# Four edits to the order of the work in a gated mix of dilated attention and a squared-ReLU MLP

## The chip, the cores and the metric

The kernel runs on one core of one Trainium2 chip. A core has a matrix engine (TensorE, PE in the profile, whose weight loads are shown apart as PEld), a vector engine (VectorE, DVE), a scalar engine (ScalarE, ACT), GpSimd (POOL), and SyncE (SP), which here does nothing but issue the transfers (DMAs) between the memories. The metric is the time of one launch on the device in microseconds (us), the median of several runs.

## What is computed

The input x has 2,048 rows (tokens) of 448 numbers. One branch is attention with 16 heads of 28 numbers, in which a token sees itself and seven earlier ones at every second place; the other is an MLP with 1,792 hidden columns and a squared ReLU. A gate per token mixes them:

```python
qkv = (x @ wqkv).reshape(B, S, 3, H, Dh)               # H = 16, Dh = 28
off = jnp.arange(8) * 2                                # a window of 8, dilation 2
logits = einsum("bhsd,bhswd->bhsw", q, k[s - off]) * Dh ** -0.5
a = einsum("bhsw,bhswd->bhsd", softmax(logits), v[s - off]) @ wo
h = x @ w1 + b1
b = relu(h) ** 2 @ w2 + b2
g = sigmoid((x * gate_w).sum(-1))
out = g * a + (1 - g) * b
```

All of it is float32, and so are the operands on TensorE. Each operand is split into a high part that is rounded (ScalarE writes it) and a low part, the difference (VectorE subtracts). A product is then three: high by high, high by low, low by high.

## The kernel before

**Tiling and stages.** The tokens are taken in four chunks of 512. First comes the product with wqkv, chunk by chunk, which also makes the sum under the gate as one more column of v. Chunk 0 is `qkv_first`. Chunk 1 is two calls of `qkv_two`, one for each two tiles of 128 tokens. Chunk 2 is `qkv_seven`, which makes q and k by seven products where eight are usual; it needs sums and differences of the chunk's tokens, which `token_sums(2)` makes on VectorE and then splits into parts. Chunk 3 is again two calls of `qkv_two`, and into the second of them the first products of the MLP (h) are put. Then the MLP runs over the chunks in the order 3, 0, 1, 2 (products called h and b), and the product with wo closes the attention.

**Row halves.** The inner dimension is cut into halves of 64 rows. Two products, one of the lower and one of the upper 64 rows, run side by side on TensorE, each into its own accumulator (a bank of PSUM); 63 such pairs make one call of `qkv_two`. When both accumulators of two such products are through with their first half, they change places: what ran in the lower rows now runs in the upper. Before that, `turn` makes VectorE write one element into each of the two banks (L212), in a column that holds no result. The write waits for the products so far and the next products wait for the write, so it sets the halves' order. In `qkv_two` the list of steps says after how many pairs each turn stands. In chunk 2 the function `turned` (L360) writes in the same way.

**What sets the order.** No scheduler chooses; the program is written under `tc.manual_schedule()`, and instructions go to each engine's queue in the order in which Python issues them. That order follows a planned clock. `advance(dt)` adds the planned time of some products to `clock["pe"]` and then issues whatever is due: `when(t, fn)` puts work at a planned time of the whole run, `at(dt, fn)` at a time from now, and `soon` is 1,500 ns from now (`LO_DELAY`), used for low parts, which so go to VectorE some time behind ScalarE's high part. Planned times (in ns) are not measured ones: each engine takes its queue in order and waits for what it needs.

**Attention** is a generator with its own planned clock, which `advance` keeps beside that of the products. It has eight units: two halves of the tokens (par) by four groups of four heads (g). For a unit, GpSimd makes eight products of q and k (`qk_piece`, L561), and VectorE sums each over a head's 28 numbers (L562); after the softmax GpSimd makes eight products with v (L568), and VectorE sums them (L576). GpSimd's products go through four buffers in turn (`PP_BUFS`). The unit's q, k and v are loaded from memory (`att_load_qk`, L532 and L533, and `att_load_v`, L538), to which `stage_store` (L235) has written them after ScalarE's copies of the accumulators into the staging tiles st (L243). After unit 0's loads, the generator lets `ATT_DELAY` ns of planned time pass.

**MLP weights.** W1 comes in four pieces. `w1_piece(i, dt, gap)` has SyncE load a piece into one of the two buffers `w1raw` (L754), and places the splits of its four parts at the planned times dt, dt + gap and so on. Pieces 0 and 1 are split straight (L130 on ScalarE, L131 on VectorE) into w1ah and w1al, and the last, short part into w17h and w17l. Pieces 2 and 3 (w1bh, w1bl) and the first rows of W2 (`w2_piece`, w2ah, w2al) go another way: ScalarE writes the high part (L740) and a copy of the raw rows into a PSUM bank (L741), and VectorE subtracts from that copy (L746). There is one copy tile, so ScalarE's next copy waits for VectorE's subtraction.

**SyncE** issues all transfers in one queue. An issue that waits (a store for its st tile, a load for the store before it) holds back all that stand behind it.

Of the kernel before, what the change touches and what calls it, by code (L numbers as in the profile page):

```python
# [33 lines left out]
QK_FIRST = 2130.0  # L34
AV_COST = 2000.0
SM_COST = 600.0
ATT_DELAY = 17000.0
LO_DELAY = 1500.0
HL_DELAY = 1800.0
COPY_DELAY = 1300.0  # L40
# [17 lines left out]
def gated_mix_kernel(ctx: ExitStack, tc: tile.TileContext, xT, wqkv, w1, w2, wo, b1, b2, out):  # L58
# [70 lines left out]
    def split_full(raw, hi, lo, soon=now):  # L129
        nc.scalar.activation(hi, raw, AF.Copy)  # L130
        soon(lambda: nc.vector.tensor_sub(lo, raw, f32(hi)))  # L131
# [117 lines left out]
    def full(x, acc, tl, b, ks=range(3)):  # L249
        sl, n = slice(tl * P, tl * P + P), block(b)  # L250
        r = []
        for k in ks:
            r += [(acc, x.h[k][:, sl], wqh[:, k, n]), (acc, x.h[k][:, sl], wql[:, k, n]),
                  (acc, x.l[k][:, sl], wqh[:, k, n])]
        return r

    def last(x, acc, tl, b):

        sl = slice(tl * P, tl * P + P)
        n = slice(D, D + NV) if b == 2 else slice(0, D)  # L260
        h, l = w7h[:, n], w7l[:, n]
        return [(acc, x.x7[:, sl], h), (acc, x.x7[:, sl], l), (acc, x.x8[:, sl], h)]

    def accs(c, b, tls, tags):
        return [Acc(t, f"qkv{c}_{tl}_{b}", NV if b == 2 else D) for t, tl in zip(tags, tls)]
# [43 lines left out]
    def qkv_two(x, c, t0, beside=(), copies=False):  # L309

        t1 = t0 + 1
        kinds = ("mm", "bm", "bb") if beside else ("mm", "mb", "bb")
        (q0, q1), (k0, k1), (v0, v1) = (accs(c, b, (t0, t1), tags) for b, tags in enumerate(kinds))
        if copies:
            copy_tile()

        parts = []
        for ends in (True, False):
            for one, two in (((q0, t0, 0), (k1, t1, 1)), ((q1, t1, 0), (k0, t0, 1)), ((v0, t0, 2), (v1, t1, 2))):
                r = [full(x, *o) + (last(x, *o) if ends else []) for o in (one, two)]  # L320
                parts.append(r if ends else r[::-1])
        run(c, [sum((p[r] for p in parts), []) for r in range(2)],
            [(24, [], (q0, k1)), (36, [], (q1, k0)), (42, [], (v0, v1)), (45, [(0, t0, q0), (1, t1, k1)]),
             (51, [], *beside[:1]), (54, [(0, t1, q1), (1, t0, k0)]), (57, [], *beside[1:]),
             (63, [(2, t0, v0), (2, t1, v1)])])

# [46 lines left out]
    class Group:  # L373
# [12 lines left out]
        def token_sums(self, n, j):  # L386
            a, b = sums[self.c, (None, 1, 0, 0, 1)[n]], (None, 1, 0, 1, 0)[n]
            o = (2 * self.u + b) * P if j < 2 else CH + b * P
            return tuple(t[:, o:o + P] for t in a)
# [146 lines left out]
    def att_load_v(par, g, tag="v"):  # L536
        v = kv_tile(tag, f"v{par}{g}")
        nc.sync.dma_start(v, halo_ap(v_d, par, g))  # L538
        return v
# [87 lines left out]
    def attention():  # L627
# [18 lines left out]
        for i in range(n + 1):  # L646
            if i < n:
# [5 lines left out]
                if i == 0:  # L653
                    vs[0] = att_load_v(par, g)
                    yield ATT_DELAY
                lgs[i] = smp.tile([P, NS, W, HG], F32, tag="lg", name=f"lg{i}")
# [71 lines left out]
    def copy_tile():  # L728


        assert not copy[1]
        copy[0] = ps("b", f"copy{len(later)}")
# [188 lines left out]
    def when(t, fn, *args):  # L921
        later.append((t, lambda: fn(*args)))
# [39 lines left out]
    def token_sums(c):  # L962
        raw = xraw[c]
        add, sub = nc.vector.tensor_add, nc.vector.tensor_sub

        def r(j, i):
            return raw[j].rearrange("p (u t n) -> p u t n", u=2, t=2)[:, :, i]

        def made(a):
            one, two = a, a + 1  # L970
            return [lambda: (add(r(two, 1), r(two, 1), r(one, 1)), sub(r(one, 1), r(one, 0), r(one, 1))),
                    lambda: (sub(r(one, 0), r(two, 1), r(one, 0)), sub(r(two, 0), r(two, 0), r(one, 0)))]

        def begin():
            for j in range(2):
                sums[c, j] = [halfp.tile([P, FA], F32R, tag=f"e{2 * j + n}", name=f"s{c}_{j}{'hl'[n]}")[:, 48:48 + CH + 2 * P]
                              for n in range(2)]

        def cut(j):
            split_full(raw[j], *(t[:, :CH] for t in sums[c, j]), soon)  # L980
            for u, rows in enumerate((LOW, HIGH)):
                split_full(raw[2 + j][rows, u * 2 * P:(u + 1) * 2 * P], *(t[rows, CH:] for t in sums[c, j]), soon)
        return made(0) + made(2) + [lambda: (begin(), cut(1)), lambda: cut(0)]

    def steps(t, gap, fns):
        for i, fn in enumerate(fns):
            when(t + i * gap, fn)
# [43 lines left out]
            when(t + 5000.0, lambda c: x_spill(c, xs[c]), c)  # L1031
    when(23500.0, x_more, 2)
    when(39500.0, x_more, 3)
    when(42500.0, lambda: steps(42600.0, 850.0, token_sums(2)))
    when(10500.0, x_spill, 0, x)
    when(25000.0, w1_piece, 0, 38000.0, 2000.0)
    when(44500.0, halos)
    when(46500.0, w1_piece, 1, 58500.0, 1500.0)
    when(66800.0, w1_piece, 2, 76300.0, 1400.0)
    when(67800.0, w1_piece, 3, 82000.0, 1400.0)  # L1040
    for j in range(2):
# [20 lines left out]
    qkv_first(xs[0])  # L1062
    qkv_two(xs[1], 1, 0)
    qkv_two(xs[1], 1, 2)
    st_["spilled"] = 0
    clock["on"] = True
    clock["att"] = clock["pe"] - 1.0
# [422 lines left out]
```

## Time and profile before

| | us |
|---|---|
| median of 3 runs | 414.14 (414.07 to 414.32) |
| the profiled execution | 414.31 |
| its span, from the first instruction to the last | 412.5 |
| TensorE busy | 407.3 (99%) |
| TensorE's weight loads busy | 391.0 (95%) |
| VectorE busy | 278.9 (68%) |
| GpSimd busy | 267.8 (65%) |
| ScalarE busy | 220.5 (53%) |

All times inside the span are counted from its start. Chunk 1's first half runs from 30.6 us, its second from 43.4, chunk 2 from 56.4, chunk 3's first half from 80.1; the MLP's first products (h) come in from 104.0. In a row of the timeline stand the start, the length in us, the engine, the line, the operation, the tiles (what is written, then what is read) with their shapes and types, the count of instructions that the row holds, and in brackets a wait with what ended it.

### The profile page before, as it was taken

The numbers are of one execution on the slowest core, as the hardware profiler recorded it, in microseconds if no ns is written. First come the engines' busy times: TensorE is split into PE (matmuls) and PEld (weight loads), VectorE is DVE, ScalarE is ACT, GpSimd is POOL, SyncE is SP. The second block draws the span as 40 slices with busy tenths as digits, with TensorE's granted clock in tenths as the row PEclk, the third lists the DMA queues.
The fourth block names the chain that finished last, engine by engine and source line by source line (L and its number), as shares of the span: only waits on it lengthen the run. The fifth ranks groups of instructions, "written<-read, shape, count | busy, mean of one in ns | idle before, by whom it ended". The sixth has DMA issues, their size and how long they took to land.

```text
span 412.5 us, 9366 instructions
## 1 busy us (share of the span) xinstructions
PE 407.3 (99%) x3817; PEld 391.0 (95%) x3817; DVE 278.9 (68%) x454; ACT 220.5 (53%) x498; POOL 267.8 (65%) x167
## 2 busy tenths in 40 slices
PE   8999999999999999999999999999999999999997
PEld 7999999989899998999999999999999999998996
DVE  4674865575857767686765897878676677792344
ACT  4674877476875555445565435354553254346640
POOL 0000000967699999979998898999989978950000
PEclk9999999999999999999999999999999999999999
DMA  7999899979272504654020679865136430158304
GB/s 216 359 370 330 254 373 277 371 229 328 97 252 84 207 11 171 209 184 153 2 85 0 206 235 265 242 153 153 43 136 224 193 129 0 39 154 151 108 2 180
DMA packets 67020, 74.00 MB, mean 179 GB/s; under 512 B 33504, under 2 KB 59296, under 8 KB 66848
## 3 DMA queue, kind: packets, MB, share of 16 engines
q1 hardware_dynamic: 66976, 73.39, 55.7%
q8 instruction: 30, 0.49, 0.5%
q14 instruction: 14, 0.11, 0.1%
HBM read 45.94 MB, written 28.25 MB: 180 GB/s over the span
## 4 chain that ended last, share of the span: by engine, by line
PE 93%; DVE 3%; DMA 1%; ACT 1%; issue 1%; SPq 0%; DVEq 0%; ACTq 0%
PE h L202 32%; PE b L202 31%; PE qkv L202 15%; PE a L202 7%; PE v L344 2%; PE qkv L291 2%; PE x L344 1%; DVE lg L562 1%; DMA xraw<-xT 1%; PE a L1262 1%; PE z L344 1%; DVE st L437 1%; PE y L344 1%; PE w L344 1%; DVE o L576 0%
## 5 line engine op out<-in xcount | busy, mean ns | idle before, releaser
L561 POOL TENSOR_TENSOR qk<-q,k 128x896 f32<-128x896 f32 x64 | 134.7, 2139 | 86.5 <-DMA k<-k_d 76.9
L568 POOL TENSOR_TENSOR av<-lg,v 128x896 f32<-128x896 f32 x64 | 118.9, 1963 | 3.2 <-DVE lg L562 2.8
L860 DVE TENSOR_TENSOR h<-h,h 128x512 fp32r<-128x512 f32 x56 | 38.6, 689 | 61.3 <-ACT h L863 60.8
L202 PE MATMUL b<-w2ah,h 64*128 64x448 f32 x448 | 74.6, 359 | 0.0
L202 PE MATMUL b<-w2bh,h 64*128 64x448 f32 x448 | 73.2, 360 | 0.4 <-DVE h L860 0.4
L576 DVE TENSOR_REDUCE o<-av 128x112 f32<-128x896 f32 x64 | 66.7, 1069 | 0.9 <-POOL av L568 0.9
L562 DVE TENSOR_REDUCE lg<-qk 128x32 f32<-128x896 f32 x64 | 67.0, 1074 | 0.0
L202 PE MATMUL qkv<-wqh,x 64*128 64x448 f32 (+1 forms) x384 | 61.6, 362 | 0.6 <-DVE qkv L212 0.6
L861 ACT ACTIVATE h<-h,b1z 128x512 f32<-128x512 f32 x56 | 36.7, 655 | 42.9 <-PE h L202 42.9
L202 PEld LDWEIGHTS b<-w2ah,h 64*128 64x128 f32 x448 | 58.9, 184 | 0.3
L202 PEld LDWEIGHTS b<-w2bh,h 64*128 64x128 f32 x448 | 55.1, 184 | 1.6 <-DVE h L860 0.7
L202 PE MATMUL b<-w2al,h 64*128 64x448 f32 x224 | 54.7, 358 | 0.0
L202 PE MATMUL b<-w2bl,h 64*128 64x448 f32 x224 | 51.8, 359 | 0.0
L202 PEld LDWEIGHTS qkv<-wqh,x 64*128 64x128 f32 x384 | 45.4, 185 | 2.7 <-DVE qkv L212 1.1
L202 PE MATMUL qkv<-wql,x 64*128 64x448 f32 (+1 forms) x192 | 44.7, 361 | 0.0
L862 ACT ACTIVATE h<-h 128x512 fp32r<-128x512 f32 x56 | 33.5, 598 | 1.7
L202 PEld LDWEIGHTS b<-w2al,h 64*128 64x128 f32 x224 | 34.2, 184 | 0.1
L863 ACT ACTIVATE h<-h 128x512 f32<-128x512 f32 x56 | 33.3, 594 | 0.0
L202 PEld LDWEIGHTS b<-w2bl,h 64*128 64x128 f32 x224 | 31.6, 184 | 0.4
L808 ACT ACTIVATE h<-h 128x4 fp32r<-128x4 f32 (+1 forms) x35 | 7.2, 207 | 45.0 <-PE b L202 44.9
L202 PEld LDWEIGHTS qkv<-wql,x 64*128 64x128 f32 x192 | 25.5, 185 | 0.7
L243 ACT ACTIVATE st<-qkv 128x448 f32<-128x448 f32 x36 | 18.0, 542 | 11.1 <-PE qkv L202 8.0
(261 smaller groups left out, 940.1 us busy)
## 6 DMA issues: line engine op xcount, KB each, us to landing
k<-k_d SPq DMA_DIRECT2D x8, 840.0 KB, 6.1
v<-v_d SPq DMA_DIRECT2D x8, 840.0 KB, 4.9
x_d<-x SPq DMA_DIRECT2D x12, 512.0 KB, 7.6
q_d<-st SPq DMA_DIRECT2D x8, 448.0 KB, 6.5
k_d<-st SPq DMA_DIRECT2D x8, 448.0 KB, 6.2
w1raw<-w SPq DMA_DIRECT2D x4, 896.0 KB, 9.7
q<-q_d SPq DMA_DIRECT2D x8, 448.0 KB, 3.6
o_d<-o SPq DMA_DIRECT2D x16, 224.0 KB, 2.7
```

The source lines that it names most:

```text
L202: nc.tensor.matmul(acc.pt[:, :acc.n], a[rows], w[rows], start=acc.todo == acc.all, stop=acc.todo == 1)
L243: nc.scalar.activation(st[:, :, t % 2], heads(pt), AF.Copy)
L291: nc.tensor.matmul(acc.pt[:, :D], a, w, start=k == j == 0, stop=False)
L344: nc.tensor.matmul(self.pt[:, :self.n], a, w, start=new, stop=True, skip_group_check=True)
L561: nc.gpsimd.tensor_mul(pr, q[:, s:s + 1].to_broadcast([P, W, C]), k[:, s:s + W])
L562: pending.append(lambda: nc.vector.tensor_reduce(lg[:, s], pr.rearrange("p w (h d) -> p w h d", h=HG), axis=AX.X, op=ALU.add))
L568: nc.gpsimd.tensor_mul(pr.rearrange("p (h d) w -> p w h d", h=HG), lg[:, s][:, :, :, None].to_broadcast([P, W, HG, DH]), v[:, s:s + W].rea ...
L576: nc.vector.tensor_reduce(o[:, g * C:(g + 1) * C], pr, axis=AX.X, op=ALU.add)
L860: nc.vector.tensor_sub(hl, pt, f32(hh))
L861: ops += [lambda pt=pt, r=r: nc.scalar.activation(pt, pt, AF.Relu, bias=b1t[:, f + r:f + r + 1]), lambda pt=pt, hh=hh: nc.scalar.activatio ...
L862: lambda pt=pt, hh=hh: nc.scalar.activation(hh, pt, AF.Square),
L863: lambda pt=pt, r=r, low=low: (nc.scalar.activation(pt, pt, AF.Square), at(delays[r], low))]
```

## The change

Four edits, none of which adds or removes an instruction:

1. `ATT_DELAY` falls from 17,000 to 16,000 ns: attention's plan runs 1 us ahead of where it was, against the products.
2. In `qkv_two` the turn of q1 and k0 stands after 30 pairs, not 36. The products themselves keep their places.
3. `token_sums` now returns two lists: the sums, which stay at 42,600 ns and every 850 from there, and the splits (`cut`), which were the last two steps of that row (46,000 and 46,850) and now stand at 50,300 and 51,700.
4. The second piece of W1 is no longer put at 46,500 ns. It is called after the second `qkv_two` of chunk 1, so that its transfer stands behind that half's stores of q, k and v. Its splits keep their planned times (58,500 and every 1,500).

```diff
--- before.py
+++ after.py
@@ -34,7 +34,7 @@
 QK_FIRST = 2130.0
 AV_COST = 2000.0
 SM_COST = 600.0
-ATT_DELAY = 17000.0
+ATT_DELAY = 16000.0
 LO_DELAY = 1500.0
 HL_DELAY = 1800.0
 COPY_DELAY = 1300.0
@@ -320,7 +320,7 @@
                 r = [full(x, *o) + (last(x, *o) if ends else []) for o in (one, two)]
                 parts.append(r if ends else r[::-1])
         run(c, [sum((p[r] for p in parts), []) for r in range(2)],
-            [(24, [], (q0, k1)), (36, [], (q1, k0)), (42, [], (v0, v1)), (45, [(0, t0, q0), (1, t1, k1)]),
+            [(24, [], (q0, k1)), (30, [], (q1, k0)), (42, [], (v0, v1)), (45, [(0, t0, q0), (1, t1, k1)]),
              (51, [], *beside[:1]), (54, [(0, t1, q1), (1, t0, k0)]), (57, [], *beside[1:]),
              (63, [(2, t0, v0), (2, t1, v1)])])
 
@@ -980,7 +980,7 @@
             split_full(raw[j], *(t[:, :CH] for t in sums[c, j]), soon)
             for u, rows in enumerate((LOW, HIGH)):
                 split_full(raw[2 + j][rows, u * 2 * P:(u + 1) * 2 * P], *(t[rows, CH:] for t in sums[c, j]), soon)
-        return made(0) + made(2) + [lambda: (begin(), cut(1)), lambda: cut(0)]
+        return made(0) + made(2), (lambda: (begin(), cut(1)), lambda: cut(0))
 
     def steps(t, gap, fns):
         for i, fn in enumerate(fns):
@@ -1031,11 +1031,15 @@
             when(t + 5000.0, lambda c: x_spill(c, xs[c]), c)
     when(23500.0, x_more, 2)
     when(39500.0, x_more, 3)
-    when(42500.0, lambda: steps(42600.0, 850.0, token_sums(2)))
+
+    def sums_begin():
+        made, cuts = token_sums(2)
+        steps(42600.0, 850.0, made)
+        steps(50300.0, 1400.0, cuts)
+    when(42500.0, sums_begin)
     when(10500.0, x_spill, 0, x)
     when(25000.0, w1_piece, 0, 38000.0, 2000.0)
     when(44500.0, halos)
-    when(46500.0, w1_piece, 1, 58500.0, 1500.0)
     when(66800.0, w1_piece, 2, 76300.0, 1400.0)
     when(67800.0, w1_piece, 3, 82000.0, 1400.0)
     for j in range(2):
@@ -1062,6 +1066,7 @@
     qkv_first(xs[0])
     qkv_two(xs[1], 1, 0)
     qkv_two(xs[1], 1, 2)
+    w1_piece(1, 58500.0, 1500.0)
     st_["spilled"] = 0
     clock["on"] = True
     clock["att"] = clock["pe"] - 1.0
```

TensorE's queue is the same as before. On GpSimd one low part of W2 stands behind the third of attention's products with v instead of ahead of it. VectorE's, ScalarE's and SyncE's queues differ at many places; the three below are those of the following text.

**SyncE, end of chunk 1.** The rows L1015 are stores of zeros ahead of the tokens, L754 is the second piece of W1, L235 are the stores of the second half of chunk 1 (each holds two token tiles), L532 and L533 the loads of q and k for attention's unit 0. Before:

```order
L1015 DMA v_d<-halo_128 8x7x112
L754 DMA w1raw_844<-w 128x4x448
L235 DMA q_d<-st_2_0_861 128x4x224
L235 DMA k_d<-st_3_1_863 128x4x224
L235 DMA v_d<-st_2_2_911 128x4x224
L532 DMA q_917<-q_d 128x896
L533 DMA k_918<-k_d 128x1680
```

Now:

```order
L1015 DMA v_d<-halo_128 8x7x112
L235 DMA q_d<-st_2_0_849 128x4x224
L235 DMA k_d<-st_3_1_851 128x4x224
L235 DMA v_d<-st_2_2_900 128x4x224
L754 DMA w1raw_906<-w 128x4x448
L532 DMA q_908<-q_d 128x896
L533 DMA k_909<-k_d 128x1680
```

The piece has moved past three stores; the loads of attention's unit 0 stand behind all four in both. On ScalarE, in the same stretch, the splits of the sums (s_1h, s_0h, three rows each) stood ahead of the first copy of q; now s_1h stands behind the four copies of q and k, and s_0h behind the two of v.

**VectorE, chunk 3, first half.** The MEMSET rows in twos are turns; the names qkv_1_0, qkv_0_1 and so on give the token tile and then 0, 1 or 2 for q, k or v. L746 is a low part made from the copy tile, L562 a sum of attention. Before:

```order
L746 TENSOR_TENSOR w17l<-copy_1275,w17h 64x64
L746 TENSOR_TENSOR w1bl_1329<-copy_1275,w1bh_1326 128x448
L562 TENSOR_REDUCE lg_1169<-qk_4_1333 128x32
L212 MEMSET qkv_1_0_1270 1x1
L212 MEMSET qkv_0_1_1271 1x1
L746 TENSOR_TENSOR w1bl_1327<-copy_1275,w1bh_1324 128x448
L562 TENSOR_REDUCE lg_1169<-qk_5_1347 128x32
L212 MEMSET qkv_0_2_1273 1x1
L212 MEMSET qkv_1_2_1274 1x1
```

Now:

```order
L746 TENSOR_TENSOR w17l<-copy_1275,w17h 64x64
L562 TENSOR_REDUCE lg_1159<-qk_4_1333 128x32
L212 MEMSET qkv_1_0_1270 1x1
L212 MEMSET qkv_0_1_1271 1x1
L746 TENSOR_TENSOR w1bl_1329<-copy_1275,w1bh_1326 128x448
L746 TENSOR_TENSOR w1bl_1327<-copy_1275,w1bh_1324 128x448
L562 TENSOR_REDUCE lg_1159<-qk_5_1347 128x32
L212 MEMSET qkv_0_2_1273 1x1
L212 MEMSET qkv_1_2_1274 1x1
```

The turn of q1 and k0 has moved past one low part. Ahead of v's turn stand the same rows as before.

**VectorE, chunk 3, second half.** Here the low parts are those of W2's first rows (w2al), and the sum of qk_0 is the first of attention's unit 1. Before:

```order
L212 MEMSET qkv_2_0_1488 1x1
L212 MEMSET qkv_3_1_1491 1x1
L746 TENSOR_TENSOR w2al<-copy_1494,w2ah 128x448
L562 TENSOR_REDUCE lg_1169<-qk_7_1405 128x32
L212 MEMSET qkv_3_0_1489 1x1
L212 MEMSET qkv_2_1_1490 1x1
L746 TENSOR_TENSOR w2al<-copy_1494,w2ah 128x448
L212 MEMSET qkv_2_2_1492 1x1
L212 MEMSET qkv_3_2_1493 1x1
L746 TENSOR_TENSOR w2al<-copy_1494,w2ah 128x448 x2
L562 TENSOR_REDUCE lg_1441<-qk_0_1547 128x32
```

Now:

```order
L212 MEMSET qkv_2_0_1488 1x1
L212 MEMSET qkv_3_1_1491 1x1
L212 MEMSET qkv_3_0_1489 1x1
L212 MEMSET qkv_2_1_1490 1x1
L746 TENSOR_TENSOR w2al<-copy_1494,w2ah 128x448 x2
L562 TENSOR_REDUCE lg_1159<-qk_7_1405 128x32
L562 TENSOR_REDUCE lg_1441<-qk_0_1547 128x32
L212 MEMSET qkv_2_2_1492 1x1
L212 MEMSET qkv_3_2_1493 1x1
L746 TENSOR_TENSOR w2al<-copy_1494,w2ah 128x448 x2
```

The turn of q1 and k0 now stands ahead of the first low part. The two sums stand together between the second low part and v's turn, where there was one between the first and the second low part and one behind the fourth.

## The prediction

> **What bounds the kernel now.** I read the page first, then the waits of the weight loads on TensorE, then single stretches of the timeline where those waits lie.
>
> ```profile
> span 412.5 us, 9366 instructions
> PE 407.3 (99%) x3817; PEld 391.0 (95%) x3817; DVE 278.9 (68%) x454; ACT 220.5 (53%) x498; POOL 267.8 (65%) x167
> ```
>
> TensorE (PE) is busy 407.3 of 412.5 us. The change leaves its 3,817 products alone, word for word in the same order, so it can move the time only through the holes between them. The profiled execution took 414.31 us, 1.8 us more than its span and 0.17 us above the median of 414.14; I add shifts of the span to the median. What TensorE's weight loads waited for, from the whole span:
>
> ```profile
> PEld qkv L202 <- DVE qkv L212: 1.1, 2, 0.9
> PEld b L202 <- DVE h L860: 0.7, 1, 0.7
> PEld h L202 <- ACT st L243: 0.2, 1, 0.2
> ```
>
> Inside the span there are four small holes: two behind VectorE's one-element writes (L212, the "turns" that the change moves), one behind a low part of the MLP at 371 us, one behind a copy at 104 us. That is the ground on which the change can gain. For the two turns:
>
> ```profile
> 30.63 0.42 PE L202 MATMUL qkv<-wqh,x 64*128 64x448 f32 x2
> ...
> 43.36 0.42 PE L202 MATMUL qkv<-wqh,x 64*128 64x448 f32 x2
> ...
> 56.41 0.37 PE L344 MATMUL v<-wqh,x 64*128 64x450 f32 x2
> ...
> 88.99 0.37 PE L202 MATMUL qkv<-wqh,x 64*128 64x448 f32 x2
> 89.92 0.47 PE L202 MATMUL qkv<-wqh,x 64*128 64x448 f32 x2 [0.56 <-DVE qkv L212]
> 90.22 0.37 PE L202 MATMUL qkv<-wql,x 64*128 64x448 f32 x2
> ```
>
> The first half of chunk 1 takes 43.36 - 30.63 = 12.73 us, the second, with the same products, 56.41 - 43.36 = 13.05: its hole costs 0.3. At 89 us a pair follows each 0.20 us; the pair due at 89.19 runs as from 90.02 (its successor is at 90.22): 0.83 lost. So 1.1 us hang on the two late turns.
>
> **The change, part by part.**
>
> *The turn of q1 and k0, six pairs sooner.* In chunk 1 it now stands before a 0.62 us low part and two sums, and nothing waits: 0.3 us gained there. In chunk 3's first half this is VectorE's row of work, with the product that follows:
>
> ```profile
> 86.36 1.13 DVE L746 TENSOR_TENSOR w17l<-copy,w17h 64x128 fp32r<-64x128 f32 x4
> 88.17 0.62 DVE L746 TENSOR_TENSOR w1bl<-copy,w1bh 128x448 fp32r<-128x448 f32 x1 [0.68 <-ACT copy L741]
> 88.71 1.08 DVE L562 TENSOR_REDUCE lg<-qk 128x32 f32<-128x896 f32 x1
> 89.72 0.64 DVE L746 TENSOR_TENSOR w1bl<-copy,w1bh 128x448 fp32r<-128x448 f32 x1
> 89.78 0.06 DVE L212 MEMSET qkv<- 1x1 f32 x2
> 90.29 1.07 DVE L562 TENSOR_REDUCE lg<-qk 128x32 f32<-128x896 f32 x1
> 91.31 0.64 DVE L746 TENSOR_TENSOR w1bl<-copy,w1bh 128x448 fp32r<-128x448 f32 x1
> 91.37 0.06 DVE L212 MEMSET qkv<- 1x1 f32 x2
> ...
> 91.83 0.36 PE L202 MATMUL qkv<-wqh,x 64*128 64x450 f32 x2
> ```
>
> The turn ended at 89.84 and TensorE went on as from 90.02, so 0.18 us pass from one to the other. Now the low part (w1bl) goes behind the turn: the reduction runs from 87.50, the turn at 88.6, due by 89.19 - 0.18 = 89.01. That hole closes, 0.83. But v's turn, the second pair of writes at 91.37, still stands behind the same instructions: the reduction (to 88.55), the turn, w1bl (to 89.2), ScalarE's refill of the one copy tile (0.6, to 89.8), w1bl (to 90.4), a reduction (1.0), so it ends at 91.50, against 91.43 now. v's products, then due 0.83 sooner, start at 91.50 + 0.18 = 91.68 instead of 91.83. The gain here is 0.15, not 0.83; VectorE's queue hands it back 1.8 us later.
>
> *Token sums' splits behind the copies.* ScalarE now copies q and k first, which lets their stores go about 1 us sooner:
>
> ```profile
> 53.42 1.38 ACT L130 ACTIVATE s_0h<-xraw 128x512 fp32r<-128x512 f32 x3
> 54.82 2.39 ACT L243 ACTIVATE st<-qkv 128x448 f32<-128x448 f32 x5
> ...
> 55.21 1.47 DVE L131 TENSOR_TENSOR s_0l<-xraw,s_0h 128x512 fp32r<-128x512 f32 x3
> ...
> 60.11 0.36 PE L344 MATMUL v<-wqh,x 64*128 64x450 f32 x2
> ```
>
> The last four of the moved rows end up behind v's copies, so near 59.3 rather than 54.8, and VectorE's low parts (1.47 us) near 59.9. Queued behind them is the turn of chunk 2's first v, due at 60.11 - 0.3 - 0.18 = 59.6. I price that at 0.3 us, between nothing (if ScalarE is 0.3 sooner) and 0.5; it eats the gain of chunk 1's turn. It does not enter the sum, because the next part fixes TensorE's place anew.
>
> *The second piece of W1 behind the stores.* The costly part. SyncE's issues, and the time to landing of the piece issued at 53.70:
>
> ```profile
> 53.70 0.60 SPq L754 DMA_DIRECT2D w1raw<-w  x1
> ...
> 57.75 1.61 SPq L235 DMA_DIRECT2D v_d<-st  x1
> 64.29 0.33 SPq L532 DMA_DIRECT2D q<-q_d  x1
> 65.65 0.33 SPq L533 DMA_DIRECT2D k<-k_d  x1
> 66.98 0.32 SPq L538 DMA_DIRECT2D v<-v_d  x1
> ...
> DMA to landing us min/median/max: 9.2/9.2/9.2
> ```
>
> The three loads at 64.29, 65.65 and 66.98 each waited for one store to land. So the transfers land one after the other in the order of issue: the piece at 62.9, then q, k and v about 1.35 us apart. With the piece last, the three stores come before it and it lands near 62.9 + 3 x 1.35 = 66.9, at the most where v landed, 66.98; if v's store is smaller or overlaps, not below 66.3. I take 66.6. [...] Who waits for the piece:
>
> ```profile
> 65.19 1.51 ACT L130 ACTIVATE w1ah<-w1raw 128x448 fp32r<-128x448 f32 x3
> ...
> 65.81 0.63 DVE L131 TENSOR_TENSOR w1al<-w1raw,w1ah 128x448 fp32r<-128x448 f32 x1 [0.52 <-ACT w1ah L130]
> 66.38 1.16 DVE L437 TENSOR_TENSOR st<-y,st 128x448 f32<-128x448 f32 x2
> 67.45 0.62 DVE L131 TENSOR_TENSOR w1al<-w1raw,w1ah 128x448 fp32r<-128x448 f32 x1
> 68.20 0.06 DVE L360 MEMSET x<- 1x1 f32 x1
> ...
> 69.17 0.36 PE L344 MATMUL x<-w2ah,s_0h 64*128 64x448 f32 x2
> ```
>
> Its splits stay where they are in ScalarE's and VectorE's order. From ScalarE's start (65.19) to the end of VectorE's second low part (68.07) and the two writes that turn x's banks is 2.93 us. With a start at 66.65 the turn ends at 69.58, and TensorE goes on at 69.76 instead of 69.17: **0.6 us lost**, whatever was gained before. ScalarE's later copies (z from 68.2, x from 70.8) stay in time for that TensorE.
>
> *The plan of attention 1 us sooner, and its loads.* GpSimd's first product waits 71.3 us for k; with the stores ahead, k arrives about 1.5 us sooner. It is no bound, but unit 1's loads and the first w2 rows are issued behind its eighth product, and TensorE meets those rows at 104 us:
>
> ```profile
> 85.16 4.24 POOL L561 TENSOR_TENSOR qk<-q,k 128x896 f32<-128x896 f32 x2
> ...
> 98.54 0.58 ACT L740 ACTIVATE w2ah<-w2raw 128x448 fp32r<-128x448 f32 x1 [2.13 <-DMA w2raw<-w]
> ...
> 103.53 0.96 ACT L243 ACTIVATE st<-qkv 128x448 f32<-128x448 f32 x2
> ...
> 103.97 0.64 PE L202 MATMUL h<-x,w17h 64*128 64x512 f32 x2
> ```
>
> h's second bank is free when the copy of 103.53 is done; now that costs the 0.2 us quoted above. The eighth product needs the buffer of the fourth, whose reduction ended at 86.26, now 86.9: it ends at 89.05 instead of 89.40, and the w2 rows land 0.35 sooner. Against that, VectorE's order there has two reductions of 1.0 us between the second and third w2 low part, where it had one between the first and second. The copy tile is handed to and fro between ScalarE and VectorE: low part 2 ends at 101.45 instead of 101.78, the reductions at 103.4, low part 3 at 104.1 instead of 103.02. The copy comes 1.05 - 0.35 = 0.7 later, and so does TensorE.
>
> *The rest.* q and k of unit 5 are now loaded ahead of three x tiles; GpSimd frees them 3 us before the first tile's turn, so nothing waits. The hole at 371 us stays: VectorE's order from 357 us on is the same. Single reductions change places with MLP low parts all along; these end 4.2 us after ScalarE's start and are due at about 5.6, so one reduction of 1.07 us fits.
>
> **Sum.** The shift is +0.6 after 70 us, +0.45 after 92, +0.7 after 104, and stays: 414.14 + 0.7 = **414.8 us**, 0.17% more. A measurement of this kernel tells about 0.2% (0.83 us) from no change, so this counts as none. With the landing between 66.3 and 66.98 it is 414.5 to 415.2.
>
> **Rivals.** *The piece is later still* (slower): the load of q is issued once q's store has landed, near 63, and if the engines work on it beside the piece, up to the 1.35 us of such a transfer is added. At half of it the sum is 414.8 + 0.7 = 415.5; it counts as slower from a landing at 66.8. For it: shares of the DMA engines near full. Against it: landings in the order of issue. *The piece is in time*: then -0.3 from chunk 1 and -0.15 at 92 stay, the w2 chain still moves, and the h products start 0.15 sooner: 414.0. Against it: the sum of the four transfers does not change. *The turns do all they could* (faster): VectorE is ahead at v's turn as well, TensorE keeps 0.3 + 0.83, and 413.0 results. Against it: each instruction ahead of v's turn is still ahead of it.
>
> **Numbers.** Forecast 0.55, piece later still 0.22, piece in time 0.13, turns do all 0.08, anything else 0.02. A quarter of the first case lies above +0.83. Faster by over 0.2%: 0.09; within: 0.55; slower: 0.36. Range 413.6 to 415.7, which leaves out most of the fast case and the upper part of the late one.
>
> **What would show it.** The timeline of the changed kernel should have no hole at 52 us; ScalarE waiting for w1raw until 66.3 to 67.0 and a hole on TensorE near 69, behind L360; the hole at 89 gone and one of 0.6 to 0.7 us near 91, behind L212; GpSimd starting near 71; and a wait of 0.4 us or more behind the copy L243 near 104. I am wrong if the piece lands before 66, if no hole stands at v's turn, or if a hole over 0.3 us appears between 110 and 360 us.

## The result, and the profile after

The changed kernel took **418.59 us** (median of 4 runs, 417.65 to 420.49) against 414.13 for the kernel before beside it: 1.0113 of its time, 95% interval 1.0077 to 1.0148. It is slower by 1.1%; the forecast was 414.8 in a range of 413.6 to 415.7. The profiled execution took 418.53, with a span of 416.7. From the page of the changed kernel, its head, and from the waits of TensorE's weight loads, the rows that are new or have changed:

```profile
span 416.7 us, 9365 instructions
PE 408.5 (98%) x3817; PEld 383.5 (92%) x3817; DVE 285.8 (69%) x454; ACT 220.5 (53%) x498; POOL 268.5 (64%) x167
...
PEld x L344 <- DVE v L360: 2.6, 1, 2.6
...
PEld x L344 <- DVE x L360: 0.9, 1, 0.9
PEld v L344 <- DVE x L360: 0.7, 1, 0.7
PEld qkv L202 <- DVE qkv L212: 0.7, 1, 0.7
PEld h L202 <- DMA x2b<-x_d: 0.6, 1, 0.6
PEld h L202 <- ACT st L243: 0.5, 1, 0.5
```

TensorE is busy 1.2 us more than before, while the span is 4.2 longer: the rest is holes. VectorE is busy 6.9 us more with the same 454 instructions, so some of them take longer. One hole of 2.6 us stands behind a turn of VectorE (L360) in chunk 2. The forecast had the others up to 105 us, but not this one. The weight loads waited 2.6 us here and the products stood idle for 2.2; the products behind the hole come 2.5 us later, which is what it costs. The timeline of TensorE there:

```profile
76.87 0.37 PE L344 MATMUL v<-w7h,x 64*128 64x450 f32 x2
79.45 0.47 PE L344 MATMUL x<-w2ah,s_0h 64*128 64x448 f32 x2 [2.20 <-DVE v L360]
```

The first split of W1's second piece on ScalarE, with its wait for the landing, and the product behind x's turn:

```profile
67.33 1.51 ACT L130 ACTIVATE w1ah<-w1raw 128x448 fp32r<-128x448 f32 x3 [1.94 <-DMA w1raw<-w]
...
70.30 0.47 PE L344 MATMUL x<-w2ah,s_0h 64*128 64x448 f32 x2 [0.53 <-DVE x L360]
```

VectorE in this stretch, and GpSimd's first products:

```profile
67.94 0.63 DVE L131 TENSOR_TENSOR w1al<-w1raw,w1ah 128x448 fp32r<-128x448 f32 x1 [2.22 <-ACT w1ah L130]
...
69.55 1.19 DVE L131 TENSOR_TENSOR w1al<-w1raw,w1ah 128x448 fp32r<-128x448 f32 x2
70.16 0.06 DVE L360 MEMSET x<- 1x1 f32 x2
70.74 0.06 DVE L360 MEMSET w<- 1x1 f32 x2
70.86 8.40 DVE L131 TENSOR_TENSOR w17l<-w1raw,w17h 64x64 fp32r<-64x64 f32 x4
79.26 0.06 DVE L360 MEMSET z<- 1x1 f32 x2
...
79.29 0.07 DVE L360 MEMSET v<- 1x1 f32 x2
```

```profile
70.69 8.42 POOL L561 TENSOR_TENSOR qk<-q,k 128x896 f32<-128x896 f32 x4 [69.30 <-DMA k<-k_d]
83.17 4.23 POOL L561 TENSOR_TENSOR qk<-q,k 128x896 f32<-128x896 f32 x2 [4.06 <-DVE lg L562]
```

Four small low parts of the second piece of W1 (w17l, at most 64x128) take 8.40 us, just as long as GpSimd's four products beside them (8.42). The turns of z, x and v stand behind them.

Where the time went can be read off the starts of the same product in both timelines; TensorE's order is the same. The shift of the changed kernel against the one before, at points between the holes (times of the kernel before):

| behind | shift there (us) | step | the step in the prediction |
|---|---|---|---|
| start and chunk 0 (51 us) | +0.09 | +0.1 | 0 |
| chunk 1's turn (53) | -0.11 | -0.2 | -0.3 |
| the turn of chunk 2's first v (61) | +0.45 | +0.6 | +0.3, not summed |
| x's turn behind w1al (71) | +1.24 | +0.8 | to +0.6 in all |
| the turns behind w17l (80) | +3.70 | **+2.5** | nothing |
| turn of q1 and k0, chunk 3 (90) | +2.85 | -0.8 | -0.83 |
| v's turn, chunk 3 (93) | +3.39 | +0.5 | +0.68 |
| the copy ahead of h (105) | +3.67 | +0.3 | +0.25 |
| an x tile's reload (322) | +4.16 | +0.5 | 0 |
| last product | +4.13 | 0 | 0 |

### The profile page after: what moved, and what is told of

The parts are those of the page before. It is cut to its first block, busy times and chain, and to the rows that moved or that the text cites. A ratio compares the mean times of both kernels' runs of the same rounds, so it can differ in the third digit from the quotient of the medians.

```text
span 416.7 us, 9365 instructions
## 1 busy us (share of the span) xinstructions
PE 408.5 (98%) x3817; PEld 383.5 (92%) x3817; DVE 285.8 (69%) x454; ACT 220.5 (53%) x498; POOL 268.5 (64%) x167
## 4 chain that ended last, share of the span: by engine, by line
PE 85%; DVE 6%; DMA 4%; issue 2%; ACT 2%; SPq 0%; DVEq 0%
PE h L202 31%; PE b L202 30%; PE qkv L202 12%; PE a L202 7%; DMA w1raw<-w 2%; PE qkv L291 2%; DVE lg L562 2%; DMA x2b<-x_d 2%; DVE w17l L131 1%; DVE st L437 1%; PE warm L873 1%; PE a L1267 1%; DVE o L576 0%; DVE w1bl L746 0%; ACT copy L741 0%
## 5 line engine op out<-in xcount | busy, mean ns | idle before, releaser
L202 PE MATMUL b<-w2ah,h 64*128 64x448 f32 x448 | 73.6, 359 | 0.0
L576 DVE TENSOR_REDUCE o<-av 128x112 f32<-128x896 f32 x64 | 66.6, 1071 | 0.5 <-POOL av L568 0.3
L562 DVE TENSOR_REDUCE lg<-qk 128x32 f32<-128x896 f32 x64 | 66.8, 1074 | 0.0
L202 PEld LDWEIGHTS b<-w2ah,h 64*128 64x128 f32 x448 | 57.8, 184 | 1.3
L202 PE MATMUL qkv<-wqh,x 64*128 64x448 f32 (+1 forms) x384 | 57.9, 360 | 0.3 <-DVE qkv L212 0.3
L202 PEld LDWEIGHTS qkv<-wqh,x 64*128 64x128 f32 x384 | 37.1, 184 | 3.3 <-DVE qkv L212 0.7
L202 PE MATMUL qkv<-wql,x 64*128 64x448 f32 (+1 forms) x192 | 35.8, 360 | 0.0
L243 ACT ACTIVATE st<-qkv 128x448 f32<-128x448 f32 x36 | 18.1, 541 | 15.5 <-PE qkv L202 12.9
L202 PEld LDWEIGHTS qkv<-wql,x 64*128 64x128 f32 x192 | 18.7, 184 | 1.3
```

Source lines behind the costliest of these rows:

```text
L202: nc.tensor.matmul(acc.pt[:, :acc.n], a[rows], w[rows], start=acc.todo == acc.all, stop=acc.todo == 1)
L243: nc.scalar.activation(st[:, :, t % 2], heads(pt), AF.Copy)
L562: pending.append(lambda: nc.vector.tensor_reduce(lg[:, s], pr.rearrange("p w (h d) -> p w h d", h=HG), axis=AX.X, op=ALU.add))
L576: nc.vector.tensor_reduce(o[:, g * C:(g + 1) * C], pr, axis=AX.X, op=ALU.add)
```

## The experiments

The experiments ran in three groups of four kernels, the first (the piece, GpSimd) on one chip, the second and third on another. The kernel before took 415.75, 415.41 and 415.76 us beside them (medians of 32, 34 and 17 runs, between 414.1 and 417.7), 1.3 to 1.6 more than beside the first measurement. Each experiment is compared with the runs beside it. The expected times of the first group were counted from the first measurement, so what is to be compared is their distance from the kernel before.

### Which edit: the piece's place alone, and everything but it

The kernel before with the fourth edit alone:

```diff
-    when(46500.0, w1_piece, 1, 58500.0, 1500.0)
...
     qkv_two(xs[1], 1, 2)
+    w1_piece(1, 58500.0, 1500.0)
```

> The kernel before with the fourth edit alone. If the piece's place alone makes the loss: the piece lands near 66.8, k near 70, the four low parts w17l start near 70.4 beside GpSimd's first products and end near 79, and TensorE has holes of 0.6 us near 69 and of about 2.4 us near 76: 417.1 us (416.5 to 417.8). If it takes the sooner copies as well, GpSimd starts only after the low parts and the time is 414.7.

Measured: 418.03 us (417.08 to 418.59) against 415.75, 1.0049 (1.0033 to 1.0066). The profile shows the same row of VectorE and the same hole as with all four edits:

```profile
70.14 8.39 DVE L131 TENSOR_TENSOR w17l<-w1raw,w17h 64x64 fp32r<-64x64 f32 x4
...
69.95 8.43 POOL L561 TENSOR_TENSOR qk<-q,k 128x896 f32<-128x896 f32 x4 [68.57 <-DMA k<-k_d]
...
PEld x L344 <- DVE v L360: 2.6, 1, 2.6
...
PEld x L344 <- DVE x L360: 0.9, 1, 0.9
```

The other way round, the changed kernel with the piece back ahead of the stores:

```diff
-    w1_piece(1, 58500.0, 1500.0)
...
+    when(46500.0, w1_piece, 1, 58500.0, 1500.0)
```

> The changed kernel with its fourth edit undone: the second piece of W1 is issued ahead of the stores again, all else as changed. If the 2.5 us lost near 76 us and the 0.8 us lost near 69 us both hang on the piece's place, VectorE's four low parts w17l (L131) take 1.2 us together near 69.7 as in the kernel before, GpSimd's first product starts after them (from 72 us on), neither hole is there, and what is left is the later turn of chunk 2's first v (+0.5), the gains of the turn (-0.2 and -0.8), v's turn (+0.5) and the h products (+0.3): 414.5 us, 413.9 to 415.1. If the early copies alone are enough to bring k ahead of the low parts, the hole near 76 stays and the time is over 416.

Measured: 416.0 us (414.63 to 420.52) against 415.75, 1.0013 (0.9986 to 1.0040): no difference that can be told. VectorE's row is short again, and GpSimd starts behind it:

```profile
72.22 1.17 DVE L131 TENSOR_TENSOR w17l<-w1raw,w17h 64x64 fp32r<-64x64 f32 x4
...
74.93 12.55 POOL L561 TENSOR_TENSOR qk<-q,k 128x896 f32<-128x896 f32 x6 [73.55 <-DMA k<-k_d]
```

(The profiled execution took 420.52, the longest of the twelve. It started 2.2 us late, by the start of the same product at 12 us; so 72.22 is 70.0 and 74.93 is 72.7 in the time of the kernel before. It lost another 3.7 us near 104, where TensorE waited 1.9 us for ScalarE's copy L243 and then ran at a granted clock of 0.50 from 109 to 112 us; its mean clock was 0.996. Nothing of this lies near 69 or 76.) The piece's place is both necessary and enough for the hole near 76 and for the one near 69. The sooner copies alone do not bring k forward.

### Why the four low parts are slow: hold GpSimd back, or let it do them

The changed kernel, with GpSimd's first product made to wait for the last low part:

```diff
+        if u == 0 and s == 0:
+            nc.gpsimd.tensor_copy(pr[0:1, 0, 0:1], f32(w17l[0:1, 511:512]))
         nc.gpsimd.tensor_mul(pr, q[:, s:s + 1].to_broadcast([P, W, C]), k[:, s:s + W])
```

> The changed kernel, with one more instruction: ahead of its first product GpSimd copies one element of the last w17l, so it starts after VectorE's four low parts. If these are slow because VectorE can't read two operands from SBUF while a product of GpSimd runs, the four take 1.2 us (0.28 each) instead of 8.4, GpSimd starts near 72.2, the hole near 76 (2.5 us) is gone: 416.1 us (415.6 to 416.6). If they are slow because of transfers that land in SBUF at that time, or of ScalarE, they stay slow (over 4 us together) and the time stays at 418.5 or more.

Measured: 415.38 us (414.84 to 417.53) against 415.75, 0.9994 (0.9976 to 1.0012). As all four edits together, but for this one instruction. VectorE and GpSimd in this run:

```profile
70.64 1.17 DVE L131 TENSOR_TENSOR w17l<-w1raw,w17h 64x64 fp32r<-64x64 f32 x4
72.23 0.07 DVE L360 MEMSET z<- 1x1 f32 x2 [0.42 <-PE z L344]
...
71.95 0.17 POOL L562 COPY qk<-w17l 1x1 f32<-1x1 f32 x1 [70.56 <-DVE w17l L131]
72.20 14.65 POOL L563 TENSOR_TENSOR qk<-q,k 128x896 f32<-128x896 f32 x7
```

The piece of W1 landed at the same place in the order, ScalarE did the same, and the four low parts took 1.17 us instead of 8.40. So it is GpSimd's product beside them, not the transfers. TensorE's hole near 76 is gone. The changed kernel lies 2.7 us over the kernel before beside it (418.46, on the other chip, below), this one 0.4 under: 3.1 us between them, more than the 2.5 of the hole, and the 0.6 left is not explained by these runs. The profiled execution took 417.01, one of three of the twelve over 417: it waited 1.7 us (1.9 with the restart) for the copy near 104, which the last part comes back to.

The second way, the low parts of this piece on GpSimd itself:

```diff
-                split_full(raw[rows, 3, cols], hi, lo, soon)
+                if i == 0:
+                    split_full(raw[rows, 3, cols], hi, lo, soon)
+                    continue
+                nc.scalar.activation(hi, raw[rows, 3, cols], AF.Copy)
+                soon(lambda rows=rows, cols=cols, hi=hi, lo=lo: nc.gpsimd.tensor_sub(lo, raw[rows, 3, cols], f32(hi)))
```

> The changed kernel, with the four low parts w17l of this piece made by GpSimd itself ahead of its first product, not by VectorE. If the two engines' sharing is the cause, GpSimd takes about 0.4 us for each, its first product starts near 72.6, the turns of z, x and v go out in time and the hole near 76 is gone: 416.1 us (415.6 to 416.6). If transfers slow such subtractions whoever makes them, GpSimd takes over 1 us for each and its products start after 75.

Measured: 415.12 us (414.83 to 415.44) against 415.75, 0.9977 (0.9965 to 0.9989): a little under the kernel before. The four took 2.17 us on GpSimd (0.54 each, not 0.4), and its first product started at 71.58. The hole near 76 is gone here too. Both kernels came out under their forecast of 416.1 us, by 0.7 and 1.0; it kept 2 us for the other holes, which the times don't show.

### The changed kernel again, and its clock

> The changed kernel on the chip of the other runs, as their control. If the loss at the low parts w17l is a matter of order, it is there in each execution: the four take about 8.4 us, the hole near 77 is 2.3 to 2.6 us, and the time is 2 to 3 us over the runs in which GpSimd was held back (415.4) or took the low parts (415.1): 417.5 to 418.5. If the half microsecond lost at 321 us behind an x tile's reload was a chance of that one execution's transfers, no hole is there now.

Measured: 418.46 us (418.11 to 419.65) against 415.76, 1.0070 (1.0052 to 1.0088), 2.7 over the kernel before. The four low parts took 8.44 us again, from 70.23. No hole stood at 321 us, so the 0.5 us there does not come in each execution. Something else had been added, which the first profile did not have. In the busy time by stretches of this run (first the stretch and its length; after PE, PEld, DVE, ACT and POOL the granted TensorE clock, PEclk, then the transfers' share and GB/s):

```profile
76.00:79.00 3.00, 0.76 (x10) 0.37 (x8) 2.74 (x8) 0.00 (x0) 2.52 (x2) 1.00 0.00 0
79.00:80.00 1.00, 1.00 (x8) 0.93 (x10) 0.00 (x0) 0.03 (x1) 0.00 (x0) 0.69 0.00 0
80.00:81.00 1.00, 1.00 (x8) 0.88 (x8) 0.45 (x1) 0.96 (x2) 0.00 (x0) 0.50 0.73 149
81.00:82.00 1.00, 1.00 (x10) 0.88 (x8) 1.00 (x3) 0.00 (x0) 0.00 (x0) 0.50 1.02 391
82.00:83.00 1.00, 1.00 (x10) 0.90 (x8) 1.00 (x2) 0.00 (x0) 0.22 (x1) 0.61 1.03 392
83.00:84.00 1.00, 1.00 (x14) 0.99 (x12) 1.00 (x3) 0.00 (x0) 1.00 (x1) 1.00 1.08 376
```

Behind the hole TensorE ran at half its clock (0.50 in the rows) for some 3.4 us, and pairs of products followed each other every 0.37 us instead of 0.20. From before the hole to behind the slow stretch the shift grew by 4.1 us: 2.5 for the hole and some 1.6 for the clock. An execution's mean clock goes with it (3.4 us at half clock in 417 make 0.996): 0.996 in this profile and 1.0 in the first, 0.996 in four of the six runs of the changed kernel here, and in two of the four of the first measurement (418.65 and 420.49). With GpSimd held back or doing the low parts, 24 runs show none below 0.999. In the times the 1.6 us can't be seen: the four runs at 0.996 took 418.32 to 419.65, the two at 1.0 took 418.11 and 419.08. A hole of this size was not always followed by the half clock: behind the 2.2 us of the first profile and the 2.8 of the next section's the clock stayed at 1.00. And the half clock stood behind another hole as well, the 1.9 us near 104 in the profile without the piece's edit. What makes the clock fall behind one hole and not behind another is not shown here.

### One wait per product

The changed kernel with each low part cut into two halves of its columns: the same elements, eight instructions.

```diff
-                split_full(raw[rows, 3, cols], hi, lo, soon)
+                if i == 0:
+                    split_full(raw[rows, 3, cols], hi, lo, soon)
+                    continue
+                nc.scalar.activation(hi, raw[rows, 3, cols], AF.Copy)
+                m = (cols.stop - cols.start) // 2
+                for a in (0, m):
+                    soon(lambda r=raw[rows, 3, cols][:, a:a + m], hi=hi[:, a:a + m], lo=lo[:, a:a + m]:
+                         nc.vector.tensor_sub(lo, r, f32(hi)))
```

> The changed kernel with each of the four low parts w17l cut into two halves of its columns: the same elements in eight instructions. If a subtraction with both operands in SBUF has to wait for the end of GpSimd's product, and one passes per product, four of the eight end with one product each (8.4 us together), and the other four run free in about 0.2 us each, since GpSimd's four product buffers are full by then and their sums stand behind in VectorE's queue: about 9.2 us in all, the hole near 77 larger by 0.8 us, 0.7 to 0.9 us over the changed kernel. If each instruction pays 2.1 us, about 17 us, and 8 more. If the slowing goes by elements, 8.4 us and no difference.

Measured: 419.81 us (418.4 to 420.18) against 415.76, 1.0089 (1.0069 to 1.0110), and 1.35 over the changed kernel's runs beside it (0.7 to 0.9 expected). The group of the low parts (minimum, median and maximum of one in ns) in the changed kernel, and in the one with GpSimd held back:

```profile
L131 DVE TENSOR_TENSOR w17l<-w1raw,w17h x4: 2037/2072/2123, 70.9 to 77.2; 64x128 fp32r<-64x128 f32 x3, 64x64 fp32r<-64x64 f32 x1
```

```profile
L131 DVE TENSOR_TENSOR w17l<-w1raw,w17h x4: 223/284/287, 70.6 to 71.5; 64x128 fp32r<-64x128 f32 x3, 64x64 fp32r<-64x64 f32 x1
```

And in this one, first the timeline of both engines, then the group from the fourth low part on:

```profile
72.23 8.99 DVE L787 TENSOR_TENSOR w17l<-w1raw,w17h 64x32 fp32r<-64x32 f32 x8
...
72.08 8.33 POOL L561 TENSOR_TENSOR qk<-q,k 128x896 f32<-128x896 f32 x4 [70.69 <-DMA k<-k_d]
...
L787 DVE TENSOR_TENSOR w17l<-w1raw,w17h x5: 209/220/2107, 78.4 to 81.0; 64x64 fp32r<-64x64 f32 x5
```

Four of the eight took a product's time each, though they were half as wide, down to 64x32, and the last four 0.21 to 0.22 us: GpSimd had stopped by 80.41, since its four buffers were full and the sums that free them stood behind the low parts. So one subtraction got through per product, however small it was; GpSimd's product had begun first each time. The kernel before has the same subtraction with one operand in PSUM, and there it was not slow: its w17l of the later pieces, whose raw rows VectorE reads from a copy in PSUM (L746), take 1.13 us for four in the row at 86.36 that the prediction shows, while GpSimd's two products of 85.16 to 89.40 run.

### The other three edits, each alone

The splits of the token sums behind the copies (the third edit's lines alone):

> The kernel before with the third edit alone (splits of the token sums behind the copies). VectorE's low parts s_0l end near 60.3, the turn of chunk 2's first v goes out that late, and TensorE has a hole of about 0.5 us near 59.5. Nothing else: the low parts w17l stay clear of GpSimd, because the piece of W1 still lands first and k's transfer ends after it. Against the kernel before on the same chip: +0.3 to +0.6 us. If the sooner stores alone bring k ahead of the low parts, over +2.

Measured: 415.12 us (414.61 to 416.7) against 415.41, 0.9999 (0.9983 to 1.0014). The hole is there, with the low parts that make it:

```profile
59.30 1.47 DVE L131 TENSOR_TENSOR s_0l<-xraw,s_0h 128x512 fp32r<-128x512 f32 x3 [1.06 <-ACT s_0h L130]
60.78 0.06 DVE L360 MEMSET v<- 1x1 f32 x2
...
60.23 0.37 PE L344 MATMUL x<-wqh,x 64*128 64x448 f32 x2
60.91 0.47 PE L344 MATMUL v<-wqh,x 64*128 64x450 f32 x2 [0.32 <-DVE x L360]
```

The product due at 60.43 started at 60.91: 0.5 us, as expected. The times do not show it.

The turn after 30 pairs alone (`(36, [], (q1, k0))` to `(30, [], (q1, k0))`):

> The kernel before with the second edit alone (the turn of q1 and k0 after 30 pairs). TensorE keeps 0.2 to 0.3 us at 52 us, gains 0.84 near 89, gives back about 0.5 near 91 at v's turn; in chunk 3's second half the turn stands ahead of the first low part of W2 and holds VectorE until TensorE has done its 24th pair (about 99.0 us), but there is one sum less between the low parts than with all four edits, so near 104 it should give back 0 to 0.3. Sum against the kernel before on the same chip: -0.3 to -0.6 us. If the whole of the hole at 104 were the turn's doing, -0.1.

Measured: 415.78 us (414.54 to 418.86) against 415.41, 1.0015 (0.9996 to 1.0034); a gain was expected, and there is none. In the profile TensorE gains 0.2 at 52 us and 0.8 at 89, gives back 0.5 at v's turn, and then loses 1.3 at 104. ScalarE there, at the first split of W2's rows and at the copy that h waits for, in the kernel before and in this one:

```profile
98.54 0.58 ACT L740 ACTIVATE w2ah<-w2raw 128x448 fp32r<-128x448 f32 x1 [2.13 <-DMA w2raw<-w]
...
103.53 0.96 ACT L243 ACTIVATE st<-qkv 128x448 f32<-128x448 f32 x2
```

```profile
99.38 0.58 ACT L740 ACTIVATE w2ah<-w2raw 128x448 fp32r<-128x448 f32 x1 [3.15 <-DMA w2raw<-w]
...
104.38 0.96 ACT L243 ACTIVATE st<-qkv 128x448 f32<-128x448 f32 x2
```

In both, 5.00 us lie between the landing of these rows and the copy. The rows landed 0.84 later here, and TensorE was 0.44 sooner: 1.28, all of the loss. Of that 0.84, 0.25 is the later issue of the load (90.57 instead of 90.32); the rest is the transfer, which took 8.8 us to land instead of 8.2. What TensorE gained ahead of 104 us ran into this copy.

Attention's plan 1 us sooner, alone (`ATT_DELAY = 16000.0`):

> The kernel before with the first edit alone (attention's plan 1 us sooner). In chunk 3's second half one more sum (1.07 us) stands on VectorE between W2's first and third low parts. From the landing of W2's rows to the end of the copy L243 5.1 us pass in the kernel before, so now 6.1, and the hole near 104 grows by up to 1.0 us at the same landing: 0.5 to 1.0 us over the kernel before on the same chip. If the sum's place doesn't matter there, no difference.

Measured: 415.52 us (414.66 to 418.58) against 415.76, 1.0006 (0.9986 to 1.0025). The place was wrong. In chunk 3's first half a second sum now stands ahead of the turn of q1 and k0, and v's turn with it:

```profile
88.55 2.07 DVE L562 TENSOR_REDUCE lg<-qk 128x32 f32<-128x896 f32 x2
90.56 0.64 DVE L746 TENSOR_TENSOR w1bl<-copy,w1bh 128x448 fp32r<-128x448 f32 x1
90.62 0.64 DVE L212 MEMSET qkv<- 1x1 f32 x4
...
PEld qkv L202 <- DVE qkv L212: 2.1, 2, 1.9
```

The hole near 89 is 1.0 larger than before (1.9 against 0.9 in the waits). At 104 there was then nothing to wait for. The longer chain that was looked for there does exist, where the two sums of the full change stand: from the first split to the copy it is 5.98 us with GpSimd held back (100.16 to 106.14), one sum of 1.07 us more than 5.00.

### From the findings to a faster kernel

The kernel before, with both turns of `qkv_two` sooner in all but its last call:

```diff
-            [(24, [], (q0, k1)), (36, [], (q1, k0)), (42, [], (v0, v1)), (45, ...
+            [(24, [], (q0, k1)), (36 if beside else 30, [], (q1, k0)), (42 if beside else 38, [], (v0, v1)), (45, ...
```

> The kernel before, and in all but the last call of qkv_two the turn of q1 and k0 after 30 pairs and v's turn after 38 instead of 42, so that v's turn stands ahead of one low part and one sum on VectorE; chunk 3's second half is as before. TensorE should have no hole near 52, 89 or 91 us: 1.1 us sooner at 92. But the product h then meets the copy L243 near 104 that hangs on the landing of W2's rows; GpSimd's eighth product sets that landing and does not move, so the hole there grows from 0.2 to about 1.2 us, and the end is sooner by 0.1 to 0.3 us only. If the landing follows TensorE, the gain of 1.1 stays.

Measured: 415.19 us (413.88 to 419.15) against 415.41, 1.0003 (0.9982 to 1.0024). As the first case had it: in the profile TensorE has no hole at 52, 89 or 91 us and is 0.94 sooner, and the wait behind L243 grows to 1.5 us, so that it is 0.4 later behind 104.

The same with W2's first rows split later, so that ScalarE's first copies of q and k come ahead of two of the splits:

```diff
-    when(85500.0, w2_piece, 0, 4, 92500.0, 1400.0)
-    when(89100.0, w2_piece, 4, 3, 99700.0, 1400.0)
+    when(85500.0, w2_piece, 0, 4, 95300.0, 1400.0)
+    when(89100.0, w2_piece, 4, 3, 101100.0, 1400.0)
```

> As the run with both turns sooner, and W2's first rows split 2.8 us later in the plan (95,300 instead of 92,500; the second piece at 101,100 instead of 99,700), so that ScalarE's first two copies of q and k stand behind two, not four, splits. If the hole near 104 is the copy's place behind the splits, it is gone and the time is 1.0 to 1.3 us under the kernel before on the same chip. A rival: the touch of w1ah (L808), now behind the fourth split, is late by about 0.3 us near 106 and leaves 0.8.

Measured: **413.75 us** (413.46 to 414.69) against 415.41, **0.9967** (0.9954 to 0.9980). ScalarE's copy now waits for TensorE alone, though it got W2's rows only at 99.83:

```profile
99.83 0.58 ACT L740 ACTIVATE w2ah<-w2raw 128x448 fp32r<-128x448 f32 x1 [3.22 <-DMA w2raw<-w]
...
102.36 0.98 ACT L243 ACTIVATE st<-qkv 128x448 f32<-128x448 f32 x2 [0.28 <-PE qkv L202]
...
PEld h L202 <- ACT w1ah L808: 0.7, 1, 0.7
```

The 0.7 us is the rival's late touch of w1ah, 0.55 of it lost at 113 us. Last, the same with the second piece's splits every 3,000 ns, against that touch:

> As the run with both turns sooner and W2's first rows later, with the second piece of these rows split every 3,000 ns instead of every 1,400, so that ScalarE's touch of w1ah near 113 us stands behind two of its three splits, not three. If that touch, late by 0.55 us, was the last new hole, it is gone, and the time is 0.5 us under that run (413.75): 413.2 us, 1.2 to 1.9 us under the kernel before on the same chip. A rival: the last low part now competes with the low parts of h, and a hole comes near 125 when the products b begin; then no gain.

Measured: 413.94 us (413.79 to 414.61) against 415.76, 0.9959 (0.9943 to 0.9975). The touch is in time but for 0.2, and a wait of 0.4 us came behind a low part of W2 (b waits for w2al, L746) at 116 us. It is not told apart from the run before it. Both beat the kernel before and the changed one on this chip, by 1.7 to 1.8 and 4.5 to 4.7 us; against the 414.13 of the first measurement they would be only 0.2 to 0.4 sooner.

## Why the prediction was wrong

**The step that failed** is the end of the part on the second piece of W1, together with the sentence that GpSimd, 1.5 us sooner, "is no bound". Behind x's turn the prediction looked at ScalarE's later copies alone and found them in time; VectorE's four low parts w17l, which stand in its queue ahead of the turns of z, x and v, got no term. Both movements were in the working: W1's splits some 1.5 us later, k some 1.5 us sooner (1.3 for w17l and 2.0 measured). That they cross was not seen. VectorE and GpSimd in the kernel before:

```profile
69.52 1.17 DVE L131 TENSOR_TENSOR w17l<-w1raw,w17h 64x64 fp32r<-64x64 f32 x4
...
72.66 12.57 POOL L561 TENSOR_TENSOR qk<-q,k 128x896 f32<-128x896 f32 x6 [71.27 <-DMA k<-k_d]
```

They were 2.0 us apart (70.69 to 72.66); in the changed kernel they began at 70.86 and 70.69. And the low parts kept their price of 1.17 us, from a row in which GpSimd stood idle. Beside its products each takes a product's time, 2.1 us, which is 8.4 in all and 2.5 on TensorE, where the prediction had nothing. In the second profile a half clock adds 1.6.

**What held, by its steps.** The hole at 52 went (0.2 for 0.3). The turn of chunk 2's first v was late by 0.5 to 0.6, at the upper bound of 0 to 0.5. The piece landed at 67.3 in the first profile, 66.7 in the second and 66.6 with its edit alone, where 66.6 was forecast and 66.98 was the latest thought possible; the low end, 66.3, was not reached. From there to the product behind x's turn 2.97 us passed in the first profile (67.33 to 70.30) as well as with the edit alone (66.61 to 69.58), for 3.1 in the prediction, although TensorE stood 0.4 late ahead of it in the one and 0.3 early in the other. So the landing does fix TensorE's place anew, as forecast; TensorE went on 1.1 later in the first profile, not 0.6, because this landing came 0.7 later. The turn of q1 and k0 gained 0.84 at 89 for 0.83, and v's turn gave 0.54 of it back for 0.68, behind the same queue of VectorE. At 104 the loss was 0.3 for 0.25, by a mechanism that holds (two sums in the chain, 5.98 us instead of 5.00), though the numbers met by chance: W2's rows landed 2.0 later, the queue of VectorE waited for the turn as well, and TensorE was 3.4 late. Without the collision the sum nearly holds: with the low parts on GpSimd the last product came 0.56 us behind that of the kernel before, for 0.7 in the prediction.

**The rivals.** *The piece is later still* came true in the first profile (0.7 later, at its price of 415.5), but 3.1 us are missing from it. *The piece is in time* and *The turns do all they could* fell: every hole that they deny is in the profile. None of the cases had two engines in each other's way. The range took its upper end from the late piece; what happened fell under "anything else", with 0.02.

**What stays open.** The single edits' losses of 0.5 and 1.0 us, clear in the profiles, are not in their times, and the kernel before itself took 414.13 beside the first measurement and 415.4 to 415.8 on the chips of the experiments. The copy near 104 us would explain both. It waits for W2's first rows, and their time from issue to landing differs between executions: with the low parts on GpSimd they were issued at 89.99 and landed within 7.0 us; with GpSimd held back they were issued at 90.41, took 9.7 us, and TensorE lost 1.9 us at the copy. A late landing takes up what was lost ahead of it, and can itself make an execution longer: the one with GpSimd held back that lost the 1.9 us took 417.01 us, for a median of 415.38. But the kernel before was not profiled on these chips, so for its times this is argued, not shown. The spreads don't decide it either: the kernel that frees this copy has a narrow one (1.2 us, against 2.6 for the kernel before beside it), but the one with the low parts on GpSimd, which doesn't free it, has 0.6.

## What to carry to other kernels

When a change moves two engines' work in opposite directions, lay the new times of both side by side, for everything near, and not only along the chain that is being priced: a duration read from a row holds for the neighbours that it had there. A low part whose operands both lay in SBUF was cheap here while GpSimd rested (0.28 us) and cost a whole GpSimd product while it worked (2.1 us); one operand in PSUM (1.13 us for four), giving it to GpSimd (2.17 for four), or making GpSimd wait (1.17 for four) took that away. And a gain ahead of a copy that hung on a landing was worth nothing until that copy was moved, so look for the next wait behind the hole that is being closed.

## What the runs showed of the hardware that was not expected

- VectorE's subtraction of 64x32 to 64x128 with both inputs in SBUF took 2.0 to 2.2 us beside GpSimd's products of 2.1 us and 0.21 to 0.29 without them, one per product whatever its width; GpSimd's four products took 8.42 us beside them, as long as elsewhere (2.1 each), so VectorE alone paid; in all these rows GpSimd's product had begun first.
- Behind a hole of 2.2 us TensorE's granted clock fell to 0.50 for about 3.4 us in one profiled execution, 1.6 us on TensorE, and behind the same hole it stayed at 1.00 in another; in four of six executions the mean clock was 0.996. The clock of 0.50 also stood behind a hole of 1.9 us at another place, and behind one of 2.8 us it stayed at 1.00.
- The load of W2's first rows, at the same place of SyncE's queue, took 7.0 us at most to land in the profile with GpSimd's low parts and 9.7 with GpSimd held back, where TensorE lost 1.9 us by it.
